# Attention with a position bias: part of the bias rows to GpSimd, and four blocks split early

## The chip, the cores and the metric

One core of one Trainium2 chip runs the program. The metric is device time in microseconds of one execution; below it, a profiled execution is read.

## The reference, cut to what matters

```python
scores = scale * np.matmul(q, k.transpose(0, 1, 3, 2))       # B=2, H=8, S=576, D=64
psi_rel = np.log1p(np.abs(pos[:, None] - pos[None, :]))
psi_i = np.log1p(np.maximum(pos[:, None], 1.0))
x = (psi_rel / psi_i)[..., None]
bias = np.maximum(x @ w1 + b1, 0.0) @ w2                     # hidden 32, one bias per head
scores = scores + bias.transpose(2, 0, 1)[None]
attn = softmax(scores)                                       # over the last axis
attn_out = np.matmul(attn, v)
```

Two expert layers follow (a mixture of eight experts with a balanced gate, then an ELU feed-forward). They take most of the time and no edit touches them.

## The kernel before, in words

The attention runs in 38 steps. A step is one block (a pair of heads of one batch) and one tile of 128 query rows. The first group is blocks 0 to 3: in steps 0 to 3 the last, half tile of 64 rows (written to both halves), then tiles 0 to 3 in steps 4 to 19, where step s works on block s mod 4. Blocks 4 to 7 follow from step 20. In each step PE multiplies q and k into PSUM (`emit_qk`, one step ahead), VectorE adds the bias and takes the row maximum (`emit_ttr`, tile `et`), ScalarE takes the exponential (`emit_exp`), PE transposes the result one step later (`emit_tr`, `emit_trl`, tile `aT`), and PE multiplies by v (`av_pieces`). GpSimd adds a small constant to the sums (`emit_norm`), VectorE takes the reciprocal, ScalarE spreads it over 64 columns (`emit_spread`, tile `rb`).

The bias is built on the side, in 36 groups of 16 query rows. A group takes four "bias rows" (`bias_row`: 128 partitions are 4 query rows by 32 hidden units, the columns are distances; one add and maximum with zero from tile `U` into tile `ht`), one set of matmuls with w2 (`bias_mm`, tile `bps` in PSUM), and one eviction in two instructions (`bias_out`, tile `o`), which goes to a scratch in HBM. From there `load_bias` reads a skewed tile `bt` for a pair of heads and a query tile. All groups of a query tile must have left before its tile of bias is asked for (`bias_loads`), and no more than three finished groups of rows may wait for their matmuls.

Nothing schedules this part but strings. `PRO` is the order before step 0, `ORD_0`, `ORD_S` and `ORD_A` are the orders inside a step while bias is left, `ORD_B` is the order after that. Each engine works its own queue in the order in which the letters issue. The letters that matter: h one bias row, H a whole group of rows, M, P and W a bias matmul, o and O evictions, Q the next scores, R and S the maxima of the two heads, E and F their exponentials, T, U and V transposes and their copies, N, Z and K the sum, the reciprocal and its spread, X the evacuation of a product, a one fifth of a product, L and B bias tiles, k the next load of q or k, p one instruction of `prep`. `PICK` has 180 letters, one for each bias row and each eviction in the order of issue: a is ScalarE, d is VectorE.

A block's q and k come as f32 into a ring of six. Blocks 0 to 3 are multiplied as they are (one product of f32, seen as 8 matmuls in a step). Blocks 4 to 7 are first split by `prep` into a rounded copy (ScalarE) and the difference to it (GpSimd), and multiplied as three products (seen as 12 matmuls). `prep` begins in step 12.

Loads leave on SP's queue, which also carries the scratch and the bias tiles: q and k of block 1 ahead of step 0, of block 2 at step 0 and of block 3 at step 1 (`LQ`), and v of block s at step s (`LV`).

Of the kernel before, what the change touches and what calls it, by code (L numbers as in the profile page):

```python
# [7 lines left out]
F32 = mybir.dt.float32  # L8
# [3 lines left out]
ACTF = mybir.ActivationFunctionType  # L12
ALU = mybir.AluOpType
# [10 lines left out]
GRP = S // 16  # L24
# [5 lines left out]
NB = 2  # L30
LAG = 1
TO = [4, 0, 1, 2, 3]
QB = 5
AB = 2
BD = 1
PRO = "hhhhhPhhkhhhhhkOPHhOhPoPhhohWhhhhhoBhWhoWhhOQmhh"
LQ = [100, 101]
LS = [5, 8, 11]
LV = [0, 1, 2, 3, 19, 20, 21, 22]
BG = [19, 24, 29, 34]  # L40
SUMS = [(0, 1), (2,), (3,), (), ()]
PICK = (
    "ddaddadaadddaaaddaddddaaddddaaadddadddadddddadadaaadddaaaadaddadaaddaaadddadddddadaadddddd"
    "adadaadddddaadaaddadddaddddaddaadadddaddddaddddaadddadaaddddadaddddaadddadaaddadaddddddaad"
)
WARM = 8
PS = [[4, 12], [5, 14], [6, 16], [7, 18]]
ORD_0 = "HhhhRMohLQhhhhMEo"
ORD_S = [
    "hWMNRhoXhaaoThhhQhEhZhUaMVaaohhh",  # L50
    "XaaNhZTRaMWUaaEhhhhhhhVhohhhLoQ",
    "ZXTRNMhohUWoaahhhhhahaVEaMQ",
]
ORD_A = "pZXoThpaaRaSahUKhahMEoNVQLFMhhhh"
ORD_B = "RZXTKSNUaaLEaaaFVppgQ"
ORD_E = "XZKfTNUaafaaaV"
LR = 33
# [187 lines left out]
def attention_moe_elu_ffn_kernel(  # L245
# [14 lines left out]
    act, dve, pe, pool, sp = nc.scalar, nc.vector, nc.tensor, nc.gpsimd, nc.sync  # L260
# [894 lines left out]
    blocks = [hb for grp in groups for hb in grp]  # L1155
# [13 lines left out]
    def attention(fill):  # L1169
# [11 lines left out]
        prepped = {}  # L1181
        rawqk = {}
# [11 lines left out]
        rcs = {}  # L1194
        rbs = {}

        def load_qk(i):
            rawqk[blocks[i]] = []
            hp, b = blocks[i]
            for src, rt in ((qt, ring[0]), (kt, ring[1])):  # L1200
                r = rt[:, i % 6]
                sp.dma_start(out=r, in_=src[b, hp])
                yield
                rawqk[blocks[i]].append(r)

        def load_now(i):
            for _ in load_qk(i):
                pass

        def new_qk():  # L1210
            return [qkp.tile([128, S], F32R, tag=t, name=t) for t in ("qh", "kh", "ql", "kl")]
# [14 lines left out]
        def load_v(i):  # L1226
            hp, b = blocks[i]
            vt = vpool.tile([128, 5, 128], F32, tag="v", name="vt")
            sp.dma_start(out=vt, in_=vp[b, hp])
            vts[blocks[i]] = vt  # L1230

        prep_q = []
        picks = iter(PICK)
        nh, no = [0], [0]
# [10 lines left out]
        def prep_next():  # L1245
            while prep_q:
                try:
# [2 lines left out]
                except StopIteration:  # L1250
                    prep_q.pop(0)

        pairs = []
        for s, (hp, b, t) in enumerate(steps):
            if pairs and pairs[-1][2:] == (hp, t):
# [98 lines left out]
                else:  # L1354
                    at_q.append((dst, src))

        def emit_spread(s):
            r = rows[s]
            rbs[s] = rbp.tile([128, 128], F32, tag="rb", name="rb")
            act.activation(  # L1360
                out=rbs[s][0:r].rearrange("p (h d) -> p h d", h=2),
                in_=rcs.pop(s)[0:r].unsqueeze(2).to_broadcast([r, 2, 64]),
                func=ACTF.Copy,
            )

        def emit_trl(s):
            z = s - 1
# [105 lines left out]
        def run_step(s):  # L1473
            d = s - LAG
            cur, tr = s < NS, 0 <= d < NS
            for x in ORD_0 if s == 0 else ORD_S[s - 1] if s < 4 else ORD_A if no[0] < GRP else ORD_B if cur else ORD_E:
                if x == "T" and tr:
                    emit_tr(d)
                elif x == "U":
                    while at_q:  # L1480
                        dve.tensor_copy(*at_q.pop(0))
                elif x == "V" and tr:
                    emit_trl(d)
                elif x == "Q" and s + 1 < NS:
                    emit_qk(s + 1)
                elif x in "RS" and cur:
                    emit_ttr(s, "RS".index(x))
                elif x in "EF" and cur:
                    emit_exp(s, "EF".index(x))
                elif x == "N":  # L1490
                    if 1 <= s <= NS:
                        emit_norm(s - 1)
                elif x == "Z":
                    if 2 <= s:
                        emit_recip(s - 2)
                elif x == "K":
                    if s - 2 < NS and not two[s - 2]:
                        emit_spread(s - 2)
                elif x == "X":
                    x_evac()  # L1500
                elif x == "a":
                    av(1)
                elif x == "M":
                    bias_p()
                elif x == "W":
                    bias_p(2)
                elif x == "O":
                    bias_o()
                elif x == "o":
                    bias_o(max(len(mq) - 1, 0))  # L1510
                elif x == "H":
                    bias_hh()
                elif x == "h":
                    bias_row()
                elif x == "p":
                    prep_next()
                elif x == "g":
                    do_bg(2 if s >= NS - 2 else 1)
                elif x == "L":
                    bias_loads(s)  # L1520
                elif x == "f":
                    fill_pe(s)
            if tr:
                av_q.extend(av_pieces(d))

        U = up.tile([128, S], F32, name="U")
        bpsi = csb[:, C_PSI:C_PSI + NM]
# [17 lines left out]
        def bias_row():  # L1545
            if not part:
                if nh[0] >= GRP or len(hq) >= 3:
                    return
                g = gorder[nh[0]]
                nh[0] += 1  # L1550
                part.extend((g, max(S - 16 * g, 16 * g + 16), []))
            g, n, ht = part
            m = 4 * g + len(ht)
            h = hts[m0[0] % 12 // 3][:, m0[0] % 3]
            m0[0] += 1
            if next(picks) == "a":
                act.activation(out=h[:, 0:n], in_=U[:, 0:n], func=ACTF.Relu, bias=bpsi[:, m:m + 1])
            else:
                dve.tensor_scalar(h[:, 0:n], U[:, 0:n], bpsi[:, m:m + 1], 0.0, ALU.add, ALU.max)  # L1559
            ht.append(h)  # L1560
            if len(ht) == 4:
                hq.append((g, n, ht))
                part.clear()
# [70 lines left out]
        def bias_loads(s):  # L1634
            while nk[0] < len(pairs) and (nk[0] < NB or pairs[nk[0] - NB][1] < s):
                t = pairs[nk[0]][3]
                if no[0] < min(max(gorder.index(g) for g in range(8 * t, min(8 * t + 8, GRP))) + 1 + BD, GRP):
                    break
                load_bias(nk[0])
                nk[0] += 1  # L1640

        ld = [load_qk(1)]
        for x in PRO:
            if x == "H":
                bias_hh()
            elif x == "P":
                bias_p(1)
            elif x == "h":
                bias_row()
            elif x == "m":  # L1650
                bias_p()
            elif x == "W":
                bias_p(2)
            elif x == "o":
                bias_o(max(len(mq) - 1, 0))
            elif x == "O":
                bias_o()
            elif x == "k":
                next(ld[0], None)
            elif x == "B":  # L1660
                load_bias(nk[0])
                nk[0] += 1
            elif x == "Q":
                emit_qk(0)
        next(ld[0], None)
        for s in range(NS + LAG):
            if 100 + s in LQ:
                load_now(2 + LQ.index(100 + s))
            for i, s0 in enumerate(LS):
                if s == s0:  # L1670
                    ld[0] = load_qk(4 + i) if i < 2 else load_last()
                if s0 <= s < s0 + 5:
                    next(ld[0], None)
            if s in LV:
                load_v(LV.index(s))
            if s == LR:
                for _ in load_raw(2, slice(TOFF[4], S)):
                    pass
            for i, s0 in PS:
                if s == s0:  # L1680
                    prep_q.append(prep(i))
            if s == NS:
                left.close()
                filler = fill()
            run_step(s)
            if s >= NS:
                continue
            if s in (15, 16, 17):
                raw_load()
            if s + 1 in BG:  # L1690
                i = BG.index(s + 1)
                w_split() if i < 2 else ops_first(i - 2)
            if s == 15:
                w = csb[:, C_WG:C_WG + 4 * E].rearrange("p (k e) -> p k e", k=4)
                dve.memset(wg32, 0.0)
                dve.tensor_copy(wg32[:, :, 0:E], w)
# [85 lines left out]
```

## Time and profile before

| | |
|---|---|
| median of 3 runs | 1119.75 us (1119.35 to 1121.17) |
| profiled execution, its own time | 1121.9 us |
| its span, first to last instruction | 1120.1 us |
| PE busy / VectorE / ScalarE / GpSimd | 99% / 79% / 53% / 7% |
| granted TensorE clock | 1.00 throughout |

Busy is the time in which an engine has an instruction in work. On PE the ends of matmuls are modelled, so that a busy PE is not yet a PE at its peak.

### The profile page before, as it was taken

What the parts mean: (1) busy time and instruction counts of PE and PEld (TensorE: products, weight loads), DVE (VectorE), ACT (ScalarE), POOL (GpSimd) and SP (SyncE); (2) the same over time, 40 slices, a digit from 0 to 9 for tenths busy, and PEclk for the clock granted to TensorE, in tenths of its full rate; (3) what the DMA queues carried; (4) which work ended last, traced back from release to release, by engine and by line L of the source; (5) the groups of instructions that cost most, each with busy time, mean ns of one, the idle gap of its engine ahead of it and who ended that gap; (6) DMA issues with size and microseconds to landing.
All of it is one profiled execution on the core that took longest, in us unless ns stands there. A gap on an engine that the chain in (4) does not pass through costs nothing.

```text
span 1120.1 us, 20604 instructions
## 1 busy us (share of the span) xinstructions
PE 1105.6 (99%) x7962; PEld 968.5 (86%) x7962; DVE 884.0 (79%) x1911; ACT 598.2 (53%) x1351; POOL 73.0 (7%) x104
## 2 busy tenths in 40 slices
PE   8999999999999999999999999999999999999998
PEld 4558989899898998989989899898998887999896
DVE  7998988678788887888878888787566579888876
ACT  7998976534344443444434444343433367866663
POOL 0014640000000000000000000000000022000000
PEclk9999999999999999999999999999999999999999
DMA  6876531211223233232333323232111101021002
GB/s 211 290 224 228 158 89 58 76 39 59 94 93 114 69 110 96 93 114 68 112 96 93 113 66 114 94 95 67 57 39 38 57 20 32 24 59 38 26 14 84
DMA packets 36929, 101.37 MB, mean 90 GB/s; under 512 B 4192, under 2 KB 4320, under 8 KB 36832
## 3 DMA queue, kind: packets, MB, share of 16 engines
q1 hardware_dynamic: 36832, 100.07, 28.0%
q8 instruction: 62, 1.02, 0.4%
q14 instruction: 35, 0.29, 0.1%
HBM read 78.41 MB, written 21.64 MB: 89 GB/s over the span
## 4 chain that ended last, share of the span: by engine, by line
PE 90%; DVE 5%; DMA 3%; ACT 1%; issue 1%; POOL 0%; SPq 0%; DVEq 0%; ACTq 0%
PE y L756 43%; PE m L563 39%; PE av L1425 3%; PE sc L1295 2%; PE bps L1579 2%; DMA bt<-scr 1%; PE tr L1346 1%; DMA scr<-o 1%; DVE ht L1559 1%; DVE et L1310 1%; DMA ring<-kt 1%; DVE o L1612 0%; ACT et L1326 0%; PE av L1394 0%; DVE ol L462 0%
## 5 line engine op out<-in xcount | busy, mean ns | idle before, releaser
L563 PE MATMUL m<-oh,w1h 128*128 128x256 f32 (+1 forms) x1120 | 330.6, 295 | 1.1 <-ACT p L576 0.7
L563 PE MATMUL m<-ol,w1h 128*128 128x256 f32 (+1 forms) x1120 | 329.3, 294 | 0.1
L563 PE MATMUL m<-oh,w1l 128*128 128x256 f32 (+1 forms) x1120 | 329.0, 294 | 0.0
L756 PE MATMUL y<-w2h,hh 128*128 128x512 f32 x720 | 281.6, 391 | 0.7 <-ACT hh L670 0.6
L756 PE MATMUL y<-w2l,hh 128*128 128x512 f32 x720 | 281.5, 391 | 0.8 <-DVE w2l L462 0.8
L756 PE MATMUL y<-w2h,hl 128*128 128x512 f32 x720 | 281.5, 391 | 0.0
L563 PEld LDWEIGHTS m<-oh,w1h 128*128 128x128 f32 x1120 | 210.2, 188 | 7.8 <-ACT u L576 1.1
L563 PEld LDWEIGHTS m<-ol,w1h 128*128 128x128 f32 x1120 | 210.1, 188 | 5.6 <-DVE ol L462 0.4
L563 PEld LDWEIGHTS m<-oh,w1l 128*128 128x128 f32 x1120 | 210.4, 188 | 0.0
L576 ACT ACTIVATE u<-m 128x256 f32<-128x256 f32 (+1 forms) x160 | 65.4, 409 | 197.9 <-PE m L563 197.9
L756 PEld LDWEIGHTS y<-w2h,hl 128*128 128x128 f32 x720 | 135.2, 188 | 27.9 <-DVE hl L673 0.4
L756 PEld LDWEIGHTS y<-w2h,hh 128*128 128x128 f32 x720 | 135.2, 188 | 25.9 <-ACT hh L670 0.9
L756 PEld LDWEIGHTS y<-w2l,hh 128*128 128x128 f32 x720 | 135.2, 188 | 25.3 <-DVE w2l L462 1.1
L787 DVE SCALAR_TENSOR_TENSOR acc<-y,P,acc 128x512 f32<-128x512 f32 x126 | 94.6, 750 | 59.5 <-PE y L756 59.4
L626 ACT ACTIVATE hh<-c 128x512 fp32r<-128x512 f32 (+3 forms) x128 | 68.9, 558 | 60.4 <-DVE c L595 60.4
L629 DVE SCALAR_TENSOR_TENSOR hl<-c,hh 128x512 fp32r<-128x512 f32 (+3 forms) x128 | 77.6, 607 | 24.8 <-ACT hh L626 22.0
L576 ACT ACTIVATE p<-m 128x256 f32<-128x256 f32 (+1 forms) x160 | 65.6, 410 | 53.0 <-PE m L563 49.9
L455 ACT ACTIVATE w2h<-raw 128x512 fp32r<-128x512 f32 x80 | 48.5, 627 | 40.5 <-PE y L756 39.8
L1310 DVE CUSTOM_DVE_ANT_0 et<-sc,bt 128x576 f32<-128x576 f32 x72 | 53.5, 754 | 10.8 <-ACT et L1326 3.8
L462 DVE TENSOR_TENSOR w2l<-raw,w2h 128x512 fp32r<-128x512 f32 x80 | 53.9, 691 | 9.0 <-ACT w2h L455 9.0
L595 DVE TENSOR_TENSOR c<-u,p 128x256 f32<-128x256 f32 (+1 forms) x80 | 37.9, 473 | 25.6 <-ACT u L576 25.2
L1326 ACT ACTIVATE et<-et,nmx 128x576 f32<-128x576 f32 x72 | 55.3, 771 | 0.8 <-DVE nmx L1310 0.8
(158 smaller groups left out, 1445.1 us busy)
## 6 DMA issues: line engine op xcount, KB each, us to landing
raw<-w1p SPq DMA_DIRECT2D x32, 512.0 KB, 3.9
raw<-w2p SPq DMA_DIRECT2D x32, 512.0 KB, 3.6
scr<-o SPq DMA_DIRECT2D x36, 295.5 KB, 3.7
bt<-scr SPq DMA_DIRECT2D x16, 576.0 KB, 4.4
cw<-w1d SPq DMA_DIRECT2D x16, 512.0 KB, 4.1
wsc<-ca SPq DMA_DIRECT2D x32, 256.0 KB, 3.6
cw<-w2d SPq DMA_DIRECT2D x16, 512.0 KB, 4.1
raw<-wsc SPq DMA_DIRECT2D x16, 512.0 KB, 3.6
```

Of the source, the lines that this page charges most:

```text
L455: act.activation(out=dst(bh.get()), in_=src(), func=ACTF.Copy)
L462: lambda e: eng[e].tensor_tensor(out=dst(bl.get()), in0=src(), in1=dst(bh.get().bitcast(F32)), op=ALU.subtract),
L563: lambda e, w=w, o=o, j=j, k=k: pe.matmul(x["ap"](bank), w.get()[:, ai, j, :], o.get()[:, bi, j, :], start=(k == 0 and i in (1, 2, 5)), st ...
L576: lambda e: act.activation(out=b.get()[:, 0:N], in_=x["ap"](bank), func=ACTF.Copy),
L595: lambda e: eng[e].tensor_tensor(out=blk(b.get()[:, half * N:half * N + N], rev), in0=ap(p), in1=ap(q), op=ALU.add),
L626: op([("A", cA(w))], lambda e: act.activation(out=hh(), in_=ap(), func=ACTF.Relu), r=sk, w=wh, after=gate_)
L629: lambda e: dve.scalar_tensor_tensor(out=bl.get()[:, d], in0=ap(), scalar=0.0, in1=hhf(), op0=ALU.max, op1=ALU.subtract),
L756: lambda e, a=a, w=w, f=f, i=i, y=y, c=c: pe.matmul(y.get(), a.get()[:, c], w.get(), start=(f == 0 and i == 0), stop=(f == 3 and i == 2)),
L787: lambda e: dve.scalar_tensor_tensor(out=a.get(), in0=y.get(), scalar=P[0][:, n, e_:e_ + 1], in1=a.get(), op0=ALU.mult, op1=ALU.add),
L1310: dve.tensor_tensor_reduce(out=e.rearrange("p (x j) -> p x j", x=2), in0=sc[0:r, :, 0:HALF], in1=biast[hp, t][0:r, h].rearrange("p (x j) - ...
L1326: act.activation(out=e, in_=e, func=ACTF.Exp, scale=-1.0, bias=nmx[:, h:h + 1], accum_out=sm[:, h:h + 1])
L1425: pe.matmul(p[64 * h:64 * h + 64, o:o + r], vt[:, j - 1 if j else 4, 64 * h:64 * h + 64], a[:, 4 * h + j - 1 if j else 8, o:o + r], start= ...
```

## The change

27 of the 144 bias rows go to GpSimd (a third letter, p, in `PICK`). The letter J spreads the reciprocal on GpSimd; it stands in `ORD_A` alone. The letter G issues one of four split instructions of a block: a rounded copy on VectorE or a difference on GpSimd, for q and then for k. Block i may begin from step 1 + i on, and its scores are three products from then on. By the strings, block 0 is split in step 1, block 1 in step 2, block 2 in step 3 and block 3 in step 4; the G's of later steps do nothing. The buffer sets for split blocks go from 5 to 7. The loads of q, k and v for blocks 1 to 3 (and v of block 0) leave in one list, one for each letter k: two ahead of step 0, three in step 0, three in step 1, one each in steps 2 and 3. Two B's stand in `PRO`, where one did. All orders up to step 19 are new; `ORD_T` is the order of the steps from the end of the bias to step 19.

```diff
-QB = 5
+QB = 7
-PRO = "hhhhhPhhkhhhhhkOPHhOhPoPhhohWhhhhhoBhWhoWhhOQmhh"
-LQ = [100, 101]
+PRO = "hhhhPhhkhhhhhWohhWhhkhohhWhhooPhhhhohWBhhhWhoBhhohWQo"
+LC = [1, 2, (0,), 3, (1,), (2,), (3,)]
-LV = [0, 1, 2, 3, 19, 20, 21, 22]
+LV = [19, 20, 21, 22]
+SPLIT = 1
 PICK = (
-    "ddaddadaadddaaaddaddddaaddddaaadddadddadddddadadaaadddaaaadaddadaaddaaadddadddddadaadddddd"
-    "adadaadddddaadaaddadddaddddaddaadadddaddddaddddaadddadaaddddadaddddaadddadaaddadaddddddaad"
+    "dappdpdaadddadddaapdadaaddddapdddaaddadadddpaddpaadaapaadddadaddapddpadaddaddddaadddddpaaa"
+    "dddddadddaaddddpdappdpaddddaddpdadddpapdapaddpdadaddadpddaaddpadpddddaapadddpaadapdpdadadd"
 )
-ORD_0 = "HhhhRMohLQhhhhMEo"
+ORD_0 = "hhhhkhWkhhhhMkohRhQEo"
 ORD_S = [
-    "hWMNRhoXhaaoThhhQhEhZhUaMVaaohhh",
-    "XaaNhZTRaMWUaaEhhhhhhhVhohhhLoQ",
-    "ZXTRNMhohUWoaahhhhhahaVEaMQ",
+    "hGGGhWXGoaNThkZahhkhMhaaoRUVhkhhEQMa",
+    "hhXhhoGGhWoTGhahGMaohLRkahUNVQZhaaEhhh",
+    "hhGRThhhhNWWUMXEokoVaoGhhGGaZaaaQh",
 ]
-ORD_A = "pZXoThpaaRaSahUKhahMEoNVQLFMhhhh"
+ORD_A = "hGhGGXGZSJhhhRNhhTMaoFUaaahpLahhhhVhMEohpQ"
+ORD_T = "LZpGXKTNaRESaaUapgaFGVQ"
...
+        def split_first(s):
+            i, k = divmod(split[0], 4)
+            if i > 3 or k == 0 and s < SPLIT + i:
+                return
+            split[0] += 1
+            if k == 0:
+                sets.append(new_qk())
+            src = rawqk[blocks[i]][k // 2]
+            hi, lo = sets[i][k // 2::2]
+            if k % 2 == 0:
+                dve.tensor_copy(hi, src)
+            else:
+                pool.tensor_tensor(out=lo, in0=src, in1=hi.bitcast(F32), op=ALU.subtract)
+            if k == 3:
+                prepped[blocks[i]] = sets[i]
...
+            if on_pool:
+                pool.tensor_copy(dst, src)
+            else:
+                act.activation(out=dst, in_=src, func=ACTF.Copy)
...
-                dve.tensor_scalar(h[:, 0:n], U[:, 0:n], bpsi[:, m:m + 1], 0.0, ALU.add, ALU.max)
+                (dve if e == "d" else pool).tensor_scalar(h[:, 0:n], U[:, 0:n], bpsi[:, m:m + 1], 0.0, ALU.add, ALU.max)
...
+        def loads():
+            for x in LC:
+                if isinstance(x, int):
+                    yield from load_qk(x)
+                else:
+                    load_v(x[0])
+                    yield
```

## Rows read from the trace of the kernel before

**Rows 1.** The page, busy time, share of the span and instructions of each engine.

```profile
PE 1105.6 (99%) x7962; PEld 968.5 (86%) x7962; DVE 884.0 (79%) x1911; ACT 598.2 (53%) x1351; POOL 73.0 (7%) x104
```

**Rows 2.** Windows: stretch and length, then busy us (instructions) of each engine, clock, DMA.

```profile
5.00:20.00 15.00, 13.82 (x138) 7.12 (x140) 13.68 (x33) 11.17 (x20) 0.00 (x0) 1.00 0.47 168
20.00:44.20 24.20, 21.95 (x262) 10.46 (x262) 21.27 (x65) 21.85 (x55) 1.22 (x5) 1.00 0.89 299
44.20:87.00 42.80, 41.85 (x563) 24.34 (x559) 41.83 (x128) 40.09 (x103) 6.27 (x11) 1.00 0.77 245
98.40:111.00 12.60, 12.44 (x203) 10.90 (x202) 10.82 (x37) 11.80 (x29) 7.80 (x10) 1.00 0.61 199
```

**Rows 3.** Windows of tile ht alone: PE, PEld, then VectorE's and ScalarE's bias rows.

```profile
20.00:44.20 24.20, 10.25 (x88) 2.02 (x88) 11.55 (x31) 10.88 (x18) 1.00 0.89 299
44.20:87.00 42.80, 14.73 (x136) 2.76 (x136) 17.24 (x45) 9.25 (x15) 1.00 0.77 245
```

**Rows 4.** Windows of tile o alone: VectorE's and ScalarE's evictions, two instructions each.

```profile
20.00:44.20 24.20, 4.77 (x10) 5.80 (x14) 1.00 0.89 299
44.20:87.00 42.80, 5.76 (x12) 10.55 (x24) 1.00 0.77 245
```

**Rows 5.** Timeline of PE: the transposes that open steps 5, 13 and 14.

```profile
43.72 0.71 PE L1346 MATMUL tr<-csb,et 64*128 64x64 f32 x16
...
82.84 0.71 PE L1346 MATMUL tr<-csb,et 64*128 64x64 f32 x16
...
86.92 0.86 PE L1346 MATMUL tr<-csb,et 64*128 64x64 f32 x16
```

**Rows 6.** Chain of waits in steps with bias: start, us, what.

```profile
59.81 0.73 PE bps L1579 x8
...
70.68 1.03 PE sc L1295 x8
...
72.57 0.69 PE tr L1346 x16
...
84.79 1.04 PE bps L1579 x8
```

**Rows 7.** Chain of waits in a step without bias, split scores.

```profile
112.55 0.85 PE sc L1295 x12
113.40 0.56 PE tr L1346 x16
113.96 1.24 PE av L1425 x20
115.20 0.27 PE av L1394 x4
```

**Rows 8.** Groups of instructions by line and shape: busy us, mean ns of one.

```profile
L1332 POOL TENSOR_SCALAR rc<-sm 128x2 f32<-128x2 f32 x34 | 8.7, 256 | 48.4 <-ACT et L1326 43.0 <-PE bps L1579 4.3
L341 POOL TENSOR_TENSOR w1l<-st,w1h 128x512 fp32r<-128x512 f32 x4 | 5.1, 1284 | 0.8 <-ACT w1h L344 0.6
L1242 POOL TENSOR_TENSOR ql<-ring,qh 128x576 fp32r<-128x576 f32 x2 | 2.9, 1462 | 10.5 <-ACT qh L1240 10.5
...
L1536 DVE TENSOR_SCALAR U<-U,csb 128x576 f32<-128x576 f32 x1 | 0.5, 519 | 1.3 <-DMA U<-lext 1.3
...
L1360 ACT ACTIVATE rb<-rc 128x128 f32<-128x128 f32 x34 | 10.4, 307 | 3.9 <-DVE rc L1336 3.9
```

**Rows 9.** Chain of waits from the last eviction on.

```profile
86.84 3.58 DMA scr<-o
...
90.48 4.28 DMA bt<-scr
```

**Rows 10.** Timeline of VectorE, first maximum of step 16, idle time in brackets.

```profile
94.92 0.76 DVE L1310 CUSTOM_DVE_ANT_0 et<-sc,bt 128x576 f32<-128x576 f32 x1 [0.66 <-DMA bt<-scr]
```

**Rows 11.** Timeline of VectorE and GpSimd side by side, at 66.7 and at 923 us.

```profile
66.71 1.15 DVE L1559 TENSOR_SCALAR ht<-U,csb 128x432 f32<-128x432 f32 x3
67.25 0.65 POOL L1332 TENSOR_SCALAR rc<-sm 128x2 f32<-128x2 f32 x1 [4.34 <-ACT et L1326]
...
921.97 0.42 DVE L595 TENSOR_TENSOR c<-m,u 128x256 f32<-128x256 f32 x1
923.49 1.48 POOL L462 TENSOR_TENSOR ol<-st,oh 128x512 fp32r<-128x512 f32 x1
923.73 1.52 DVE L595 TENSOR_TENSOR c<-u,p 128x256 f32<-128x256 f32 x1
```

More of the change, by code (lines that the diff above doesn't have):

```diff
@@ L1251, in prep_next @@
                     prep_q.pop(0)
+        split = [0]
+        sets = []
+        def split_first(s):
[13 more added lines that the diff above has]
+                prepped[blocks[i]] = sets[i]
         pairs = []
@@ L1355, in emit_tr, with emit_spread @@
                     at_q.append((dst, src))
-        def emit_spread(s):
+        def emit_spread(s, on_pool=False):
             r = rows[s]
             rbs[s] = rbp.tile([128, 128], F32, tag="rb", name="rb")
[L1360 to L1364, printed above, removed]
+            dst = rbs[s][0:r].rearrange("p (h d) -> p h d", h=2)
+            src = rcs.pop(s)[0:r].unsqueeze(2).to_broadcast([r, 2, 64])
+            if on_pool:
+                pool.tensor_copy(dst, src)
+            else:
+                act.activation(out=dst, in_=src, func=ACTF.Copy)
         def emit_trl(s):
@@ L1475, in run_step @@
             cur, tr = s < NS, 0 <= d < NS
-            for x in ORD_0 if s == 0 else ORD_S[s - 1] if s < 4 else ORD_A if no[0] < GRP else ORD_B if cur else ORD_E:
+            for x in ORD_0 if s == 0 else ORD_S[s - 1] if s < 4 else ORD_A if no[0] < GRP else ORD_T if s < 20 else ORD_B if cur else ORD_E:
                 if x == "T" and tr:
@@ L1495, in run_step @@
                         emit_recip(s - 2)
-                elif x == "K":
+                elif x in "KJ":
                     if s - 2 < NS and not two[s - 2]:
-                        emit_spread(s - 2)
+                        emit_spread(s - 2, x == "J")
                 elif x == "X":
@@ L1514, in run_step @@
                     bias_row()
+                elif x == "k":
+                    next(first, None)
+                elif x == "G":
+                    split_first(s)
                 elif x == "p":
@@ L1555, in bias_row @@
             m0[0] += 1
-            if next(picks) == "a":
+            e = next(picks)
+            if e == "a":
                 act.activation(out=h[:, 0:n], in_=U[:, 0:n], func=ACTF.Relu, bias=bpsi[:, m:m + 1])
             else:
-                dve.tensor_scalar(h[:, 0:n], U[:, 0:n], bpsi[:, m:m + 1], 0.0, ALU.add, ALU.max)
+                (dve if e == "d" else pool).tensor_scalar(h[:, 0:n], U[:, 0:n], bpsi[:, m:m + 1], 0.0, ALU.add, ALU.max)
             ht.append(h)
@@ L1640, in bias_loads @@
                 nk[0] += 1
-        ld = [load_qk(1)]
+        def loads():
[5 more added lines that the diff above has]
+                    yield
+        first = loads()
+        ld = [iter(())]
         for x in PRO:
@@ L1658, in attention @@
             elif x == "k":
-                next(ld[0], None)
+                next(first, None)
+            elif x == "L":
+                bias_loads(0)
             elif x == "B":
@@ L1664, in attention @@
                 emit_qk(0)
-        next(ld[0], None)
         for s in range(NS + LAG):
-            if 100 + s in LQ:
-                load_now(2 + LQ.index(100 + s))
             for i, s0 in enumerate(LS):
@@ L1674, in attention @@
             if s in LV:
-                load_v(LV.index(s))
+                load_v(4 + LV.index(s))
             if s == LR:
```

## The prediction

> **What bounds the kernel now.** I read the page first, then the windows of the attention part, then the same windows for the bias rows and their evictions alone, then the chain of waits, and last the timeline where GpSimd works. The page shows PE as the bound of the whole program and GpSimd nearly empty [rows 1]. From step 20 on nothing that the edits touch remains, so only the first 111 us can gain or lose.
>
> The windows [rows 2] cut that part in three. From 5 to 44.2 us (bias ahead of the steps, then steps 0 to 4) VectorE is busy 34.95 of 39.2 us and ScalarE 33.02. From 44.2 to 87 (steps 5 to 13, each with two bias groups on the side) VectorE is busy 41.83 of 42.8, PE 41.85, ScalarE 40.09. From 98.4 to 111 ScalarE is full (11.80 of 12.6) and sets the period. The transposes that open steps 5, 13 and 14 start at 43.72, 82.84 and 86.92 [rows 5]: a period of (82.84 - 43.72) / 8 = 4.89 us, then 4.08 for step 13 with the last group.
>
> Is it PE or VectorE that sets 4.89? In the chain of waits a step is scores 1.03, transposes about 0.69, and two bias matmuls of 0.73 (304 columns) to 1.04 (512) [rows 6]. Without bias the rest is shown free of waits: scores 0.85 in the split form, transposes 0.56, products with v 1.24, tail 0.27, together 2.92 [rows 7]. For the 16 groups that fall in the later steps the mean width is 396 columns, so a bias matmul is 0.73 + 0.31 x 92/208 = 0.87. Two of them, unsplit scores and the rest give 1.03 + 0.56 + 1.24 + 0.27 + 1.74 = 4.84. PE's stream and VectorE's full queue therefore bound these steps together, PE by 0.05 less.
>
> **What the edits remove, add and move.** The counts come from walking the order strings and the pick string.
>
> Up to and including step 4, VectorE's bias rows go from 53 to 59, its evictions from 9 to 1, and it gets 8 split copies. A row costs 11.55 / 31 = 0.37 us [rows 3], an eviction (two instructions) 4.77 / 5 = 0.95 [rows 4]; the trace has no split copy on it, so I bound that by a mean row's 0.37 below and by the 0.52 of the one plain instruction over 576 columns above [rows 8], and take 0.45, between them. VectorE: 6 x 0.37 - 8 x 0.95 + 8 x 0.45 = -1.8 us. ScalarE: 14 rows fewer at 10.88 / 18 = 0.60, 10 evictions more at 5.80 / 7 = 0.83: -8.4 + 8.3, nothing. So the early part has the same load on both engines, and in it one more matmul group, two more evictions and all splits are done.
>
> In steps 5 on, VectorE's rows go from 45 to 33 at 17.24 / 45 = 0.38 and its evictions from 6 to 4 at 0.96 [rows 3, 4]: -6.5 us. ScalarE's rows go from 15 to 8 at 0.62, its evictions stay 12, and the seven spreads of steps 6 to 12 leave it at 0.31 each [rows 8]: -4.3 - 2.2 = -6.5 us. The bias ends in step 12, not 13.
>
> PE: steps 4 to 19 score in split form, 12 matmuls in 0.85 for 8 in 1.03 [rows 6, 7]. I count it at 0.18 a step where PE is the bound (steps 5 to 12) and at nothing in steps 13 to 19, where ScalarE's exponentials, evictions and split copies of blocks 4 to 7 cover it [rows 2].
>
> GpSimd gets 13 rows and 8 subtractions by step 4, then 14 rows and 7 spreads. A subtraction is 1.46, in the trace with the same shape [rows 8]. A row has none of its kind there. Below stands the 2-element instruction's 0.26, above a two-input subtraction of 433 columns, 0.26 + 431 x 1.03/510 = 1.13 [rows 8]; a row reads one input, and half of that slope gives 0.69, which I take. A spread lies between 0.26 and 0.51 by the same rows; 0.38. Early: 13 x 0.69 + 8 x 1.46 + 1.3 for the four or five small ones = 22 us of 39; late: 14 x 0.69 + 7 x 0.38 + 8 x 0.26 + 1.46 = 16 of 39. GpSimd has the time. Behind a late row on its queue stand the small sum instruction of the step and, through VectorE's reciprocal in the next step, the evacuation of the products; that reciprocal comes 3 us or more later, so two rows of 0.69 are covered.
>
> Moved loads: the same ten requests for q, k and v leave SP, some tens of instructions apart from where they stood, and the second bias tile is asked for ahead of step 0. DMA is at 0.89 of its engines from 20 to 44 us [rows 2], so no byte becomes cheaper; I count nothing, bounds -1 and +1 us, from the 0.66 us for which VectorE waited for a bias tile at 94.92 [rows 10], rounded up. That wait itself goes: the last bias leaves one step earlier while step 16 stays where it is, so the 3.58 + 4.28 us of write and read back [rows 9] fall under steps 13 to 15. The larger buffer set makes no wait: the sets used again belong to blocks whose last score is a step earlier.
>
> **The price of two engines side by side.** While VectorE runs a chain of rows, GpSimd's small instruction takes 0.65 us in place of 0.26, and ends when the chain does [rows 8, 11]. And while GpSimd subtracts, a 256-wide VectorE instruction with two SBUF inputs takes 1.52 in place of 0.42 [rows 11]. So the two exclude each other in both directions, at least for such pairs. The Trainium skill says it as a rule (SBUF — State Buffer, "Who interferes with whom"): copies and tensor-scalar instructions of VectorE in a two-port mode, and two-input ones, hold a port pair with GpSimd as an exclusive lock for the whole instruction, and the second one fully blocks. The trace agrees for two-input instructions on VectorE and for GpSimd behind rows; no run here shows a VectorE row behind a long GpSimd instruction. By that rule the sum would be the second rival's; without it, the next paragraph's. I take a price of nothing: early, because VectorE's chains run on while GpSimd waits, and GpSimd then fits beside its score, transpose and eviction work (which reads PSUM), and VectorE has 39.2 - 34.95 = 4.25 us idle there; late, because VectorE gets some 0.3 us a step to spare (below).
>
> **The sum.** In the later steps PE's sum falls to 4.84 - 0.18 = 4.66 and VectorE's load to at most (41.83 - 6.5) / 8 = 4.4. PE then sets the period; with the 0.05 by which 4.89 exceeds 4.84 now it is 4.71. Eight steps gain 8 x 0.18 = 1.4 us. Step 13 without bias takes 3.3 (98.4 to 111, 12.6 us, hold just under four such steps) in place of 4.08: 0.8. The wait at 94.92: 0.7. The early part: 0. Together -2.9 us. The profiled execution took 1121.9 us around its span of 1120.1, 2.1 above the median of the runs; 2.9 off the median is 1116.8.
>
> **The rivals.** (1) *Hidden*: only the split scores pay, 1.4 us, and what the bias leaves earlier is lost again in the steps that ScalarE bounds [rows 2]: 1118.3, inside the 0.2% (2.2 us) that a measurement of this kernel can tell from no change. For it speaks that ScalarE is full there; against it that step 13 is longer than its neighbours. (2) *Exclusion*: rows and subtractions lock each other out early. Then the early stretch needs, one after the other, VectorE's 59 x 0.37 + 8 x 0.45 = 25.4 us and GpSimd's 22, together 47.4 of 39.2: +8.2 us if nothing else delays or covers them, and +2.6 with rows at 0.26; after the late gain that is +5.3 and -0.3, so 1119.4 to 1125.0, middle 1122.2. It decides from an early loss of 2.9 us on, some 35% of the strict 8.2. For it speak the stretched instructions [rows 11], and that each split copy on VectorE stands directly in front of its subtraction on GpSimd, with rows behind; against it that VectorE's rows cost the same 0.37 and 0.38 in both stretches, though GpSimd worked in the second [rows 2, 3]. (3) *A late start*: two of the first four rows go to GpSimd one after the other, so the first bias matmul waits for 2 x 0.69, at most 2 x 1.13, where VectorE's three took 3 x 0.37: up to 1.2 us later, and the first write to the scratch with it. It would leave 1116.8 + 1.2 = 1118.0.
>
> **How the numbers follow.** The forecast 0.45; hidden 0.13; exclusion 0.36, of which 0.08 ends within 0.2% and 0.28 above; a late start 0.06, of which 0.02 with a price of exclusion on top. Faster by over 0.2%: 0.45; within: 0.08 + 0.13 + 0.04 = 0.25; slower: 0.30. The likeliest gives 1116.8, by itself 1113.5 to 1117.5. Its low end adds VectorE's 1.8 us of early relief and 1 us of earlier loads, and 0.5 us for step periods at PE's bare sum. The high end of the range is the strict case of exclusion, 1125.0.
>
> **What would show it.** Right: the transposes of steps 5 to 13 come every 4.7 us with VectorE no longer full; step 5 opens at 43 to 44 us; scores with 12 matmuls from step 4; no wait for a bias tile at step 16. Wrong by exclusion: VectorE rows and split copies of 0.8 to 1.8 us in steps 1 to 4, GpSimd rows over 1 us, and step 5 opening after 47 us. Wrong by the row's price: GpSimd rows over 1.1 us beside an idle VectorE, and PE's bias matmuls waiting for GpSimd.

## The result and the profile after

The changed kernel takes 1126.03 us (median of 6 runs, 1125.33 to 1127.11), the kernel before in the same session 1120.13: a ratio of 1.0053 [1.0042, 1.0063]. It is slower, by 5.9 us, and lies 1.0 us above the end of the predicted range. The profiled execution took 1125.53 us with a span of 1123.7.

The page of the changed kernel, busy time of each engine, beside [rows 1]:

```profile
PE 1105.2 (98%) x8026; PEld 969.1 (86%) x8026; DVE 892.5 (79%) x1893; ACT 594.3 (53%) x1342; POOL 137.1 (12%) x146
```

VectorE executes 18 instructions fewer than before and is busy 8.5 us longer. GpSimd gains 64.1 us for 42 instructions, 1.53 us for one. Both are prices that the prediction had set too low.

The windows of the changed kernel, over the stretches of [rows 2] (columns as there: PE, PEld, DVE, ACT, POOL, clock, DMA):

```profile
5.00:20.00 15.00, 11.81 (x117) 4.54 (x118) 11.88 (x23) 8.94 (x18) 13.45 (x6) 1.00 0.43 157
20.00:44.20 24.20, 21.12 (x188) 7.70 (x186) 24.20 (x48) 18.07 (x44) 18.59 (x14) 1.00 0.79 268
44.20:87.00 42.80, 39.66 (x602) 25.96 (x602) 42.70 (x120) 37.02 (x93) 35.71 (x35) 1.00 0.68 227
```

From 20 to 44.2 us VectorE is full to the last digit, 24.20 of 24.20, with 48 instructions where it did 65 in 21.27. GpSimd is busy for 32.04 of the first 39.2 us. The third stretch still holds early work here, as the transposes show. The timeline of TensorE, those that open steps 5, 13, 14 and 22:

```profile
52.31 0.70 PE L1367 MATMUL tr<-csb,et 64*128 64x64 f32 x16
...
90.77 0.65 PE L1367 MATMUL tr<-csb,et 64*128 64x64 f32 x16
...
93.61 0.66 PE L1367 MATMUL tr<-csb,et 64*128 64x64 f32 x16
...
117.26 0.72 PE L1367 MATMUL tr<-csb,et 64*128 64x64 f32 x16
```

Step 5 opens at 52.31 in place of 43.72 [rows 5]. Then (90.77 - 52.31) / 8 = 4.81 us a step against 4.89, and step 13 takes 2.84 against 4.08. So the loss is made before step 5, and part of it is given back behind it. From the transposes of step 38 to the end of the span it is 958.0 to 958.8 us in the profiles of before, after and all twelve kernels below, so nothing behind the attention steps differs.

How far can one profile be trusted? Five kernels below issue the same instructions up to step 5 as the kernel before; with it they open that step at 41.76, 43.61, 43.72, 44.47, 45.41 and 47.30 us. The changed kernel's 52.31 lies well outside, but a difference of 2 us in this opening says nothing by itself. The time from step 5 to step 13 is steadier: 39.08 to 39.12 us in the kernel before and three others that do the same there (row_price, order_t, subs_added).

What fills the early part, by groups of instructions of VectorE and GpSimd from 4.4 to 52.3 us (busy us, mean ns of one):

```profile
L1586 DVE TENSOR_SCALAR ht<-U,csb 128x560 f32<-128x560 f32 (+16 forms) x56 | 33.7, 660 | 0.0
...
L1268 DVE CAST kh<-ring 128x576 fp32r<-128x576 f32 x4 | 4.2, 1060 | 0.0
L1268 DVE CAST qh<-ring 128x576 fp32r<-128x576 f32 x4 | 2.0, 510 | 0.0
...
L1586 POOL TENSOR_SCALAR ht<-U,csb 128x528 f32<-128x528 f32 (+9 forms) x13 | 26.6, 2052 | 6.9 <-DVE U L1562 4.2 <-PE bps L1606 2.6
L1270 POOL TENSOR_TENSOR kl<-ring,kh 128x576 fp32r<-128x576 f32 x4 | 6.2, 1542 | 3.2 <-DVE rc L1357 2.4 <-DVE kh L1268 0.8
L1270 POOL TENSOR_TENSOR ql<-ring,qh 128x576 fp32r<-128x576 f32 x4 | 6.0, 1511 | 2.2 <-DVE qh L1268 2.1
```

and VectorE's rows of the kernel before, from 4.4 to 43.72 us:

```profile
L1559 DVE TENSOR_SCALAR ht<-U,csb 128x560 f32<-128x560 f32 (+16 forms) x53 | 21.3, 458 | 0.4 <-PE bps L1579 0.3
```

A VectorE row takes 0.66 us as a mean of the recorded times, where it took 0.46; by busy time, in which overlapping ends count once, 33.7 / 56 = 0.60 against 21.3 / 53 = 0.40. A GpSimd row takes 2.05. Rows and copies of VectorE are 33.7 + 6.2 = 39.9 us of the 47.9; GpSimd's rows and subtractions 26.6 + 12.2 = 38.8. Both engines are taken for some four fifths of this part by these alone. An instruction that is held up counts as busy.

The chain of waits of the changed kernel in that part (start, us, what):

```profile
4.61 1.34 POOL ht L1586
5.95 1.24 issue
7.19 4.32 POOL ht L1586 x2
...
27.97 5.11 DMA scr<-o
...
33.43 1.68 DVE kh L1268
35.11 2.21 DVE ht L1586 x3
...
47.07 1.59 DVE kh L1268
```

It begins on GpSimd's rows, and from 33.1 to 59.2 us all its pieces are VectorE's, apart from issue. The timeline of the changed kernel beside one of these copies shows why it is so long:

```profile
33.09 0.42 DVE L1586 TENSOR_SCALAR ht<-U,csb 128x416 f32<-128x416 f32 x1
...
33.25 1.54 POOL L1270 TENSOR_TENSOR ql<-ring,qh 128x576 fp32r<-128x576 f32 x1 [1.04 <-DVE qh L1268]
33.43 1.68 DVE L1268 CAST kh<-ring 128x576 fp32r<-128x576 f32 x1
```

The subtraction starts behind the q copy and ends at 33.25 + 1.54 = 34.79. The k copy of VectorE, begun at 33.43, ends at 35.11, 0.32 us after it. The q copies, which stand ahead of a subtraction, take 0.51.

### The profile page after: what moved, and what is told of

Its sections match the earlier page's. It is cut to its first block, busy times and chain, and to the rows that moved or that the text cites. A ratio compares the mean times of both kernels' runs of the same rounds, so it can differ in the third digit from the quotient of the medians.

```text
span 1123.7 us, 20764 instructions
## 1 busy us (share of the span) xinstructions
PE 1105.2 (98%) x8026; PEld 969.1 (86%) x8026; DVE 892.5 (79%) x1893; ACT 594.3 (53%) x1342; POOL 137.1 (12%) x146
## 4 chain that ended last, share of the span: by engine, by line
PE 90%; DVE 5%; ACT 1%; DMA 1%; issue 1%; POOL 1%; SPq 0%; DVEq 0%; ACTq 0%
PE y L758 42%; PE m L565 39%; PE av L1447 3%; PE sc L1316 2%; PE bps L1606 2%; DVE ht L1586 2%; PE tr L1367 1%; ACT et L1347 1%; POOL ht L1586 1%; DVE et L1331 0%; DMA scr<-o 0%; PE av L1416 0%; DVE ol L464 0%; DMA bt<-scr 0%; DVE c L669 0%
## 5 line engine op out<-in xcount | busy, mean ns | idle before, releaser
L364 POOL TENSOR_TENSOR st<-xt,xt 128x256 f32<-128x256 f32 x4 | 3.3, 822 | 738.1 <-ACT oh L457 735.4
```

## The experiments

All times are ratios to the kernel before on the same chip in the same session. For orientation, 0.0010 is 1.1 us.

**Rows without anyone waiting for them, and the change taken apart.** Four kernels ran together (kernel before 1121.3).

rows_twice, on the kernel before; TWICE holds the places of the change's 27 rows:

```
+            if m0[0] - 1 in TWICE:
+                pool.tensor_scalar(dm[0][:, 0:n], U[:, 0:n], bpsi[:, m:m + 1], 0.0, ALU.add, ALU.max)
```

> The kernel before; beside 27 of its bias rows (those of the same number in order of issue as the changed kernel's 27) GpSimd computes the same row into a tile that nobody reads. Nothing is taken from VectorE or ScalarE, and nobody waits for GpSimd. Exclusion (GpSimd's long instructions stall VectorE's rows): slower by 3 to 12 us, VectorE's mean row well above 0.44 us. Slow rows (the harm is that PE waits for GpSimd's rows): no change within 1 us, VectorE's rows as before. Orders: no change.

Measured 1.0033 [1.0017, 1.0048]. The groups of its bias part (0 to 160 us):

```profile
L1562 DVE TENSOR_SCALAR ht<-U,csb 128x512 f32<-128x512 f32 (+17 forms) x98 | 46.0, 514 | 0.2
L1564 POOL TENSOR_SCALAR dm<-U,csb 128x304 f32<-128x304 f32 (+14 forms) x27 | 50.6, 1873 | 6.7 <-DVE U L1539 4.3
```

In the kernel before VectorE's rows are, over the same time:

```profile
L1559 DVE TENSOR_SCALAR ht<-U,csb 128x512 f32<-128x512 f32 (+17 forms) x98 | 38.9, 444 | 0.4 <-PE bps L1579 0.3
```

The same 98 VectorE rows take 46.0 us where they took 38.9: (46.0 - 38.9) / 27 = 0.26 us of VectorE's time are lost for each GpSimd row, though nothing reads it. The exclusion is there, and a GpSimd row takes 1.87 us. The waits of this kernel, as of subs_added and the two halves below, show no engine waiting for GpSimd up to 110 us.

rows_back, on the kernel after: the 27 rows are VectorE's again.

```
-    "dappdpdaadddadddaapdadaa...
+    "dadddddaadddadddaaddadaa...
```

> The changed kernel with the 27 rows back on VectorE; split, loads and orders stay. Exclusion: VectorE gets 27 x 0.4 = 10.8 us more of its own work and loses the stalls behind 27 rows of 1.9 us; its rows fall from 0.59 us to 0.44 to 0.47 (8 subtractions still stall some), time 1121 to 1125. Slow rows: PE's waits for GpSimd (8 us) go, VectorE's 10.8 us come, 1126 to 1129. Orders: 1126 as it was, or above.

Measured 1.0026 [1.0015, 1.0037]; step 5 opens at 49.35. About half of the loss of 0.0053 goes with the rows.

no_split, on the kernel after: blocks 0 to 3 aren't split early, steps 4 to 19 score as before.

```
         def split_first(s):
+            return
```

> The changed kernel without the early split of blocks 0 to 3 (8 copies on VectorE and 8 subtractions on GpSimd left out, scores of steps 4 to 19 from one f32 product as before); rows, loads and orders stay. Exclusion: the stalls behind 8 subtractions of 1.5 us go (the copies of 1.7 us shrink away too), some 6 to 10 us early, and 8 to 16 x 0.18 us on PE come back: 1118 to 1123. Slow rows or orders: only PE's 1.4 us come back, 1127.

Measured 1.0016 [1.0005, 1.0028]; step 5 opens at 49.21. 0.0053 - 0.0016 = 0.0037 go with the split. The median of 1123.46 us is 0.5 above the range that I expected of exclusion, and far from the 1127 of its rivals. By these ratios the split carries more than the rows (0.0037 against 0.0027), but each is known to about 0.0015 only, and part of the time of no_split is lost by the clock (last section).

orders_alone, on the kernel after: both together, and the spreads back on ScalarE. The orders, the loads and the seven split buffers remain.

```
-ORD_A = "hGhGGXGZSJhhh...
+ORD_A = "hGhGGXGZSKhhh...
```

> The changed kernel with no row, no split and no spread on GpSimd: only the new orders, loads, both bias tiles ahead and the larger buffer set remain. Exclusion or slow rows: both are gone; 1118 to 1123, step 5 opening near 44 us. Orders (the new order itself is the cost): 1125 to 1128, step 5 opening near 52 us.

Measured 0.9999 [0.9990, 1.0008]; step 5 opens at 44.29. Orders and loads by themselves change the time by less than 0.0010 either way. Against this kernel the rows cost 0.0017 and the split 0.0027, each with the spreads on GpSimd, both together 0.0054; that this is more than their sum lies inside the intervals.

**The price of a row and of a subtraction, by themselves.**

row_price, on the kernel before:

```
+            for n in {21: (576, 432, 304), 23: (576, 576)}.get(s, ()):
+                pool.tensor_scalar(dm[0][:, 0:n], U[:, 0:n], bpsi[:, 0:1], 0.0, ALU.add, ALU.max)
+            for n in {22: (576, 432, 304), 23: (576,) * 4}.get(s, ()):
+                dve.tensor_scalar(dm[1][:, 0:n], U[:, 0:n], bpsi[:, 0:1], 0.0, ALU.add, ALU.max)
```

> The kernel before with rows that nobody reads behind step 21: three on GpSimd (576, 432 and 304 columns), three on VectorE behind step 22, and behind step 23 two on GpSimd beside four on VectorE, all of 576. Slow engine: a GpSimd row with nothing beside it takes 1.1 to 1.5 us at 576 columns and some 0.7 us at 304, and the 1.9 us in the kernel after are its time and not a wait. Exclusion: the same GpSimd row takes 0.7 to 0.8 us where VectorE reads no tile of SBUF at the time and over 1.2 us beside VectorE's rows, and a VectorE row that begins behind a GpSimd row is recorded at 1 us or more against 0.6 us alone.

It was run once, for these rows and not for its time. Its groups of GpSimd from 114 to 119.7 us, and its windows of these rows alone, one for each (VectorE's busy time, then GpSimd's):

```profile
L1691 POOL TENSOR_SCALAR dm<-U,csb 128x576 f32<-128x576 f32 x1 | 2.2, 2230 | 0.0
L1691 POOL TENSOR_SCALAR dm<-U,csb 128x432 f32<-128x432 f32 x1 | 1.7, 1735 | 0.1
L1691 POOL TENSOR_SCALAR dm<-U,csb 128x304 f32<-128x304 f32 x1 | 1.3, 1298 | 0.1
```

```profile
114.07:116.30 2.23, 0.99 (x2) 2.23 (x1) 1.00 0.85 277
116.30:118.23 1.93, 0.85 (x2) 1.74 (x2) 1.00 0.67 245
118.23:119.60 1.37, 0.00 (x0) 1.29 (x1) 1.00 0.00 0
```

The row of 304 columns has nothing beside it, VectorE is idle from 117.86 to 119.86 in the timeline: 1.30 us. The other two lie on a line with it, (2.23 - 1.30) / 272 = 3.4 ns a column, with VectorE's rows beside part of them. The recorded times hold by the starts too: this row and the one behind it in the queue begin 1.39 us apart. So GpSimd's row is slow by itself, slower than either expectation had it (some 0.7 us for 304 columns alone). VectorE adds less: by that line the 13 early rows of the changed kernel, 464 columns on average, would take 1.85 us, and they take 2.05. In the other direction, the timeline of the same kernel where four VectorE rows of 576 columns meet GpSimd:

```profile
121.57 1.28 POOL L341 TENSOR_TENSOR w1l<-st,w1h 128x512 fp32r<-128x512 f32 x1
...
121.81 1.37 DVE L1693 TENSOR_SCALAR dm<-U,csb 128x576 f32<-128x576 f32 x1
...
122.83 4.81 POOL L1691 TENSOR_SCALAR dm<-U,csb 128x576 f32<-128x576 f32 x2
...
123.21 0.88 DVE L1693 TENSOR_SCALAR dm<-U,csb 128x576 f32<-128x576 f32 x1
...
124.12 0.52 DVE L1693 TENSOR_SCALAR dm<-U,csb 128x576 f32<-128x576 f32 x1
...
124.68 0.89 DVE L1693 TENSOR_SCALAR dm<-U,csb 128x576 f32<-128x576 f32 x1
...
125.36 2.29 POOL L1691 TENSOR_SCALAR dm<-U,csb 128x576 f32<-128x576 f32 x1
```

The row that begins 0.24 us behind a subtraction takes 1.37 us and ends 0.33 us after it. The one at 124.12, in the middle of a GpSimd row, takes 0.52 and pays nothing; those at 123.21, soon after a GpSimd row began, and at 124.68, over the end of that row and the start of the next, take 0.88 and 0.89. Two prices, then: a two-input subtraction stops a VectorE row until it ends; a GpSimd row costs it some 0.37 us about its start, and lets it run afterwards. The Trainium skill (SBUF — State Buffer, "Who interferes with whom") has the second engine blocked fully for the whole instruction, where VectorE's is a copy or tensor-scalar in a two-port mode. The subtraction agrees with that; the GpSimd row doesn't, since a VectorE row begins and ends inside it at full speed.

subs_added, on the kernel before, two in each of steps 1 to 4:

```
+                elif x == "Y" and s < 5:
+                    pool.tensor_tensor(out=dm[0], in0=U, in1=U, op=ALU.subtract)
```

> The kernel before with eight subtractions of 128 x 576 on GpSimd added, two in each of the steps 1 to 4, whose result nobody reads; VectorE's and ScalarE's work is as before. Exclusion: each of the eight, at about 1.5 us as its split shows it, holds up VectorE for part of its time, so step 5 opens 2 to 5 us after the 43.72 us of before and the time is 2 to 4 us longer. Side by side (the split's price is its copies alone): step 5 opens within 0.5 us of before and the time is the same within 1 us.

Measured 1.0026 [1.0015, 1.0036], step 5 at 45.64. Its groups (0 to 160 us):

```profile
L1563 DVE TENSOR_SCALAR ht<-U,csb 128x512 f32<-128x512 f32 (+17 forms) x98 | 42.7, 479 | 0.0
L1520 POOL TENSOR_TENSOR dm<-U 128x576 f32<-128x576 f32 x8 | 9.2, 1154 | 5.0 <-DVE U L1540 4.4
```

(42.7 - 38.9) / 8 = 0.48 us of VectorE's rows are lost for one subtraction; taken row by row, five of the rows are 0.68 to 0.99 us longer than in the kernel before and the others the same within 0.12. Eight subtractions without a single copy already cost about what the split costs over the new orders (0.0027). The opening of step 5 adds nothing to that: it lies among those of kernels without these subtractions. What the copies add isn't shown: no run has them alone, and the split also shortens the scores.

**Does a row cost the same everywhere?**

twice_early and twice_late, on rows_twice: the first 13 duplicates alone, or, with [13:], the last 14.

```
-            if m0[0] - 1 in TWICE:
+            if m0[0] - 1 in TWICE[:13]:
```

> The kernel before with the first 13 of the 27 unread duplicate rows on GpSimd alone, those up to step 5. Theory (the two engines hold each other up, and it costs only where VectorE's work sets the pace, which is the early part): it carries 2.5 to 3.5 us of the 4.4 us that all 27 cost. Rival (each row costs the same wherever it stands): 13 of 27 of 4.4, that is 1.8 to 2.4 us.

> The kernel before with the last 14 of the 27 unread duplicate rows alone, those from step 5 on. Theory: 0.5 to 1.5 us slower than before. Rival (the same price everywhere): 2.0 to 2.6 us slower.

Measured 1.0021 [1.0012, 1.0029] and 1.0029 [1.0019, 1.0039]. My theory of a price in the early part alone falls: late duplicates cost no less. VectorE's rows in the two kernels, in that order:

```profile
L1562 DVE TENSOR_SCALAR ht<-U,csb 128x512 f32<-128x512 f32 (+17 forms) x98 | 43.5, 488 | 0.4 <-PE bps L1584 0.3
L1562 DVE TENSOR_SCALAR ht<-U,csb 128x512 f32<-128x512 f32 (+17 forms) x98 | 40.9, 462 | 1.3 <-PE bps L1584 1.2
```

Early they grow to 43.5 us, (43.5 - 38.9) / 13 = 0.35 for each GpSimd row; late to 40.9, 0.14 for each. More than half of the late growth is a single row, in the timeline of twice_late in step 12:

```profile
77.13 4.38 POOL L1564 TENSOR_SCALAR dm<-U,csb 128x496 f32<-128x496 f32 x2
...
83.49 1.44 POOL L1245 TENSOR_TENSOR ql<-ring,qh 128x576 fp32r<-128x576 f32 x1 [1.98 <-ACT qh L1243]
83.68 1.53 DVE L1562 TENSOR_SCALAR ht<-U,csb 128x512 f32<-128x512 f32 x1
...
85.94 1.91 PE L1298 MATMUL sc<-ring 64*128 64x288 f32 x8
```

Two duplicates hold GpSimd's queue for 4.38 us, but the subtraction of block 4's split doesn't wait for them: GpSimd stands idle for 1.98 us before it, for ScalarE's copy. What has changed is what it meets. A VectorE row begins 0.19 us behind it and takes 1.53 us, 1.05 more than the same row in the kernel before; the maxima behind that row are late, and the scores, which wait for them, take 1.91 us where they take 1.19 elsewhere in this kernel. Step 12 is 0.98 us longer than before, and the eight steps from 5 on together 2.33 (41.45 against 39.12). So the late price is exclusion too, where VectorE is full, and nearly half of it comes from a subtraction that was there before. The two ratios together make 0.0050, the 27 rows at once 0.0033; the intervals are too wide to tell whether that is a difference.

**Is anything won behind step 5?**

late_rows, on the kernel after: no early split, the 13 rows ahead of step 5 back on VectorE; 14 late rows and the spreads stay on GpSimd.

```
-    "dappdpdaadddadddaapdadaa...
+    "dadddddaadddadddaaddadaa...
         def split_first(s):
+            return
```

> The kernel after without the split of blocks 0 to 3 in the early steps, and with the 13 GpSimd rows of the steps before step 5 given back to VectorE; the 14 later rows and the spread stay on GpSimd. Theory (what is placed before step 5 costs, what is placed behind it gains): step 5 opens near the 44.3 us of the new orders alone, a step with bias takes about 4.82 us against 5.07, and the time is 1 to 3 us below that of the new orders alone, at 1118 to 1120 us. Rival (a GpSimd row costs about what it saves wherever it is): a step takes 5.0 us or more and the time is 1120 to 1122 us.

Measured 0.9994 [0.9985, 1.0003]. Steps 5 and 13 open at 44.38 and 83.57, in orders_alone at 44.29 and 84.84. 39.19 us for the eight steps against 40.55: the late rows and spreads gain 1.36 us in place, 4.90 a step against 5.07, between the two expectations. Against no_split, 0.0016 - (-0.0006) = 0.0022 are the price of the 13 early rows, 2.5 us. The time over orders_alone is 0.0005 lower, inside the intervals.

order_t, on the kernel before: the new order of the steps without bias up to 19, less its split letters.

```
+ORD_T = "LZpXKTNaRESaaUapgaFVQ"
-            for x in ORD_0 if s == 0 else ORD_S[s - 1] if s < 4 else ORD_A if no[0] < GRP else ORD_B if cur else ORD_E:
+            for x in ORD_0 if s == 0 else ORD_S[s - 1] if s < 4 else ORD_A if no[0] < GRP else ORD_T if s < 20 else ORD_B if cur else ORD_E:
```

> The kernel before with one thing of the change: the new order for the steps without bias up to 19. Theory (that order takes 0.27 us off each step from 14 to 19): these steps take 3.03 us against 3.3, step 22 opens 1.5 to 2 us before the 113.23 us of before, and the time is 1 to 2 us shorter, at 1119 to 1120 us. Rival (the gain is taken back behind step 19): step 22 opens earlier, but the time is within 0.5 us of before.

Measured 0.9992 [0.9984, 1.0001]. Step 22 opens at 110.56, but this execution was 1.55 us ahead at step 1 already (22.99 against 24.54). From the opening of step 5 to that of step 22 it takes 68.80 us, the kernel before 69.51. That the 0.7 us are the order's isn't shown: row_price, which keeps the old order up to there, takes 68.75.

order_t_rows, on order_t: 15 late rows (in the pick string the first and last of steps 5 to 11 and the first of step 12) and the spreads on GpSimd.

```
-ORD_A = "pZXoThpaaRaSahUKhahMEoNVQLFMhhhh"
+ORD_A = "pZXoThpaaRaSahUJhahMEoNVQLFMhhhh"
```

> The kernel before with the new order for the steps without bias up to 19, and on GpSimd 15 bias rows of the steps 5 to 12 (the first and the last of a step) and the spread of the reciprocals there; nothing before step 5 is changed. Theory (gain behind step 5): step 5 opens at 43.7 us, a step with bias takes 4.65 to 4.8 us against 4.89, and the time is 1 to 2 us below that of the new late order alone, at 1117 to 1119 us. Rival (rows cost what they save): 4.85 to 4.95 us a step, and the time of the late order alone within 0.7 us.

Measured 0.9993 [0.9984, 1.0002], no gain over order_t; steps 5 to 13 take 39.94 us. Step 12 eats what the others win. Its timeline of GpSimd, and what TensorE meets behind it:

```profile
78.31 2.00 POOL L1562 TENSOR_SCALAR ht<-U,csb 128x512 f32<-128x512 f32 x1 [0.29 <-PE bps L1582]
80.28 1.44 POOL L1243 TENSOR_TENSOR ql<-ring,qh 128x576 fp32r<-128x576 f32 x1
81.64 0.51 POOL L1364 COPY rb<-rc 128x128 f32<-128x128 f32 x1
```

```profile
82.20 0.28 PE L1396 MATMUL trl<-csb,rb 64*128 64x64 f32 x1 [1.00 <-POOL rb L1364]
```

A row of 2.00 us, the subtraction and the spread stand in one queue, and TensorE waits 1.00 us for the last. A VectorE row that begins at 80.48, beside the subtraction, takes 1.52 us here as well; step 12 takes 6.31 us against 5.09.

rows_no_spread, on order_t_rows: the spread on ScalarE again, and the last two of the 15 rows on VectorE.

```
-ORD_A = "pZXoThpaaRaSahUJhahMEoNVQLFMhhhh"
+ORD_A = "pZXoThpaaRaSahUKhahMEoNVQLFMhhhh"
```

> As the kernel before with the late order and the late rows, but the spread stays on ScalarE and the last two GpSimd rows (end of step 11, start of step 12) are VectorE's again: 13 rows. Theory (the spread behind a GpSimd row of 2.0 us and a subtraction made TensorE wait 1.0 us in step 12): that wait is gone, step 13 opens 1 us or more earlier after step 5 than with the spread on GpSimd, and the time is 1118.3 to 1119.7 us, 0.5 to 1.5 us below the late order alone. Rival (the rows gain nothing): 1119.8 to 1120.6 us.

Measured 0.9989 [0.9979, 0.9999], a median of 1119.33: the fastest of all kernels here, and the only one whose interval lies below the one of before. Steps 5 and 13 open at 45.41 and 84.09: 38.68 us for the eight steps, 1.26 less than with the spread and the two rows on GpSimd, and 0.44 less than before. Step 12 takes 5.09 us again; whether the spread or the two rows had cost it, this run doesn't tell. In time it is 0.0011, or 1.2 us, below the kernel before; from order_t (0.9992) the intervals don't separate it.

## Why the prediction was wrong

The step that failed first is the price of a GpSimd row, "half of that slope gives 0.69, which I take", with 1.13 as its upper bound. It measured 1.90 us as a mean of the 27, 2.05 for the early ones, and 1.30 us for 304 columns beside an idle VectorE. I had taken a one-input instruction to cost less than a two-input subtraction; it costs more: 2.23 against 1.15 to 1.46 for 576 columns. With it falls "GpSimd has the time": not 22 us of 39 but 26.6 + 12.2 + 1.2 = 40.0 of 47.9 early.

The step that failed with it is "I take a price of nothing" for two engines side by side. VectorE's rows went from 0.40 to 0.60 us of busy time early, its k copies took 1.06 where I had 0.45. I took "VectorE: ... = -1.8 us" for the early part; up to step 5 VectorE was busy for 44.74 us in place of 34.70, so 10.0 us more, which covers the 8.6 us by which step 5 came later. Rows and copies took 39.9 us, not 25.4. rows_twice, twice_early and subs_added show this price with nobody waiting for GpSimd: 0.35 us for an early row, 0.48 for a subtraction. An early GpSimd row takes from VectorE about what it was to save it, 0.35 against 0.37, and leaves its own two microseconds as a delay. In the changed kernel that delay shows among the waits from 4 to 53 us:

```profile
PEld bps L1606 <- DVE ht L1586: 7.5, 16, 1.4
PEld bps L1606 <- POOL ht L1586: 5.4, 4, 2.1
```

The three causes, a slow row, VectorE held up, TensorE waiting for GpSimd, aren't separated in microseconds for the changed kernel; the runs separate rows from split (taken off singly, 0.0027 and 0.0037 go). One part of the "price of nothing" held: VectorE's work that reads PSUM runs beside a subtraction at its own speed. In the trace of before a maximum at 79.14 and a copy of transposes at 84.23 begin inside one and take 0.75 and 0.69 us, as elsewhere.

**The rivals.** Exclusion was the right one, in place and in sign, and its marks stood as written: two of the four k copies of 1.7 us, GpSimd rows over 1 us, step 5 behind 47 us. Its strict case, +8.2 us early, is near what the profile shows against the same orders (52.31 - 44.29 = 8.0), but by luck: it added VectorE's 25.4 and GpSimd's 22, while in truth each took about 40 side by side. The wrong row's price showed too, all its marks: over 1.1 us beside an idle VectorE, and TensorE waiting. A late start was real: the first eviction comes at 10.63 in place of 8.72, 1.9 us later, over the 1.2 that I gave it; with the same orders and the rows on VectorE it comes at 8.02 (rows_back). I gave exclusion 0.36 where the traces of before already had its two witnesses [rows 11]; "VectorE's rows cost the same 0.37 and 0.38 in both stretches" was no evidence against it, since GpSimd was busy for only 6.27 of the second 42.8 us [rows 2].

**The later steps.** The period of 4.71 was 4.81, 0.08 a step under the 4.89 where I had 0.18. Scores do come in split form from step 4. VectorE was not relieved as far as I had it (37.65 us busy of the 38.46 between steps 5 and 13, by its rows' 16.18 / 37 = 0.44 us in place of 0.38). The new order of the bias steps also costs in itself: orders_alone takes 5.07 a step, on the old order it was 4.89. Late GpSimd rows and spreads take back 0.17 of that. The 3 us or more that I gave the reciprocal behind the sum was read too wide: at 82.48 in the trace of before it comes 1.43 us behind. No wait came of it.

**Step 13 and the bias tile.** Step 13 took 2.84 in place of 4.08, more than the 0.8 that I counted; in orders_alone it takes 3.03, so most of it comes with the new orders. The wait at 94.92 [rows 10] is gone after: from 85 to 112 us no engine of the changed kernel waits for a bias tile. What it was worth is less sure than I had it, since order_t waits 1.39 us there and row_price not at all.

From step 13 to step 22 the changed kernel takes 26.49 us, the kernel before 30.39 (29.67 in row_price, which has the same orders): 3.9 us where I had 0.8 + 0.7. orders_alone takes 27.19 with neither rows nor split on GpSimd, so 3.2 of the 3.9 come with the new orders and loads; which of them does it stays open. From step 5 to step 22 it is 64.95 against 69.51, 4.6 us gained where I had 2.9 (orders_alone: 67.74). So the gain behind step 5 was larger than predicted. The early loss of 8.6 in these profiles outweighs it. These two profiles leave 4.0 us of it at step 22, the medians 5.9 at the end; the profiled execution of the kernel before is 1.8 us above its median.

## What to carry to other kernels

Work moved to an engine that stands idle is not free where the other engine reads the same memory: price both the moved instruction itself and what it does to the one it relieves, and an unread copy of it added to the old kernel shows both prices at once. Where the receiving engine has a queue of its own, look at what stands behind the moved instruction; here a 2-us row and a subtraction ahead of a spread made TensorE wait a microsecond. Look also at what runs beside it afterwards: a shifted subtraction met a row that it had missed before. An instruction never seen in the trace deserves an upper bound that is really one: a similar instruction with more inputs was none.

## What was not expected of the hardware

A GpSimd row (add of a per-partition scalar, then maximum with zero) takes 1.30 us for 304 columns and 2.23 for 576, longer than its subtraction of two tensors (1.15 for 576 in subs_added); on VectorE the same row of 576 takes 0.51.

Where TensorE had to wait early, its granted clock sometimes fell behind the wait. The windows of no_split:

```profile
5.00:8.00 3.00, 1.29 (x4) 0.28 (x4) 2.85 (x6) 2.33 (x4) 2.26 (x1) 1.00 0.44 171
8.00:11.00 3.00, 2.31 (x10) 0.47 (x12) 0.64 (x1) 0.35 (x1) 3.00 (x3) 0.56 0.00 0
11.00:14.00 3.00, 2.58 (x25) 1.00 (x25) 1.69 (x4) 0.86 (x2) 1.75 (x2) 0.87 0.00 0
```

TensorE is busy for 1.29 of 3 us, waiting for bias rows of VectorE and then of GpSimd, and then is granted 0.56 and 0.87 of its 2.4 GHz; 0.50 would be the lower of its two levels, 1.2 GHz, throughout. Of the ten runs of no_split the one at a mean clock of 1.000 took 1121.2 us, the three at 0.998 1123.3 on average, the one at 0.995 1126.0: about 1 us for each thousandth. So part of its 0.0016 is paid by the clock, which orders_alone and late_rows share (0.81 each from 26 to 35 us). Such a wait needn't lead to it: the changed kernel's profile holds 1.00 throughout these windows.
